# Output stores on ScalarE's queue and an exchange of two head pairs in the ramp: an attention and SwiGLU kernel on one core

## The chip, the cores and the metric

The kernel runs on one core of one Trainium2 chip. The metric is the device time of one execution in microseconds (us). A measurement here is six executions of a kernel, one of them with the profiler, beside eleven of the kernel before on the same chip in the same rounds (six in the first measurement of the change).

## The reference, cut to what matters

```python
# q, k, v: (8 batches, 8 heads, 576, 64); blocks of 64; w_gate, w_val: (512, 1536); w_out: (1536, 512)
scores = where(block_i >= block_j, q @ k.T / sqrt(64), -1e9)      # block-causal
attn   = softmax(scores) @ v
x      = attn as (4608 tokens, 512)
xn     = x / sqrt(mean(x * x) + 1e-6) * rms_g
out    = (silu(xn @ w_gate) * (xn @ w_val)) @ w_out                # (4608, 512) float32
```

## The kernel before

The kernel interleaves the feed-forward part of one batch with the attention of the next. The order of all work is written in strings of short names. In them `t0` to `t3` are the transposes of batch 1's head pairs on TensorE (called PE below), `a0` a set of value matmuls, `Z` a matmul of zeros whose result nobody reads and that only keeps PE busy, `U` a tile of gate or value projections, `O` a third of a down projection, `f0` to `f4` the transposes of the normalized activations by DMA, `l` a load and `p` a transpose of Q and K by DMA. In the code and in the profile, `ob` is the scaled output tile, and its scaling pass on ScalarE is called an ob below.

```python
RAMP = """
...
e3 D02 Z Z n0 Z n1 nr D11 D10 Z nx t3 Z a0 p D22 Z D12 D23 Z D20 a1 D21 D31 t0 D32 a2 D33 D30
... """
SECOND = """
... U l u1 f1 B1 u0 f0 O O C1 u2 f2 u3
f3 O l l p V00 V01 A2 l p u4 f4 V11 O V10 B3 l l l O O l l V21 l l C3 V20 z U U U U
"""
```

Each engine runs its own queue in order. SyncE (SP) issues the DMA transposes of Q and K (into tile QKT), those of the activations (XS into XT) and the output stores. A store is 128 rows of 2 KB, and there are 36.

```python
def prep(b, hp):
    ...
    sp(nc.sync.dma_start_transpose(out=T, in_=QKN[b % 2][:, hp, :, :]))       # line 258

# in Norm
def dma(self, j):
    ...
            sp(nc.sync.dma_start_transpose(out=xt(i)[:, :, lo - a:hi - a],    # line 444
                                           in_=self.XS[lo - g0:hi - g0, j, :]))

def down(i, s, part):
    ...
    for m in range(part * 4, part * 4 + 4):
        mm(po, HT[:, m, s * P:(s + 1) * P], WO[:, m, :], m == 0, m == NMC - 1)
    if part == 2:
        ob = obuf.tile([P, DM], FP32, name="ob")
        act_.mul(out=ob, in_=po, mul=0.5)
        held.discard(outs[i, s][0])
        r0 = chunks[i][0] + s * P
        sp(nc.sync.dma_start(out=out[r0:r0 + P, :], in_=ob))                  # line 557
```

A helper records all compute operations, so that in the profile all VectorE (DVE) and ScalarE (ACT) work carries line 116, all matmuls line 122 and all GpSimd loads line 102. Tiles tell them apart.

The softmax here doesn't subtract the row's maximum and nothing guards it: scores larger than these inputs give would overflow.

## Time and profile before

| | before |
|---|---|
| time, median of the first 3 executions | 377.88 us (376.99 to 378.12) |
| span of the profiled execution | 377.1 us |
| PE busy | 363.1 us, 96% |
| PE's longest DMA waits | HT 1.3 and 1.1 us (about 18 us), XT 0.5 us (82 us) |
| SyncE's queue waiting for ScalarE's ob | 123.9 us |
| mean granted clock of PE | 0.994 |

PE is the bound. A lower mean clock means that PE ran some microseconds at half speed. One stretch of 3.3 us at 0.5 lowers the mean over 377 us by 3.3 x 0.5 / 377 = 0.0044. Most of what is missing in 0.994 is one such stretch, the one at 20.8 us that the prediction shows.

### The profile page before, as it was taken

The page shows a single profiled execution, that of the slowest core. Times are in us where ns is not written, and L with a number is a line of the kernel's source. Part 1 is how long each engine was busy: PE and PEld are TensorE (multiplying, and loading weights), DVE is VectorE, ACT ScalarE, POOL GpSimd, SP SyncE. Part 2 cuts the span into 40 slices and gives each one's busy share as a digit, 9 for nine tenths or more (in the row PEclk, how much of TensorE's full clock was granted, in tenths as well). Part 3 has the DMA queues.
Part 4 walks back from the last instruction along what each step waited for, and adds up shares of the span by engine and source line. Part 5 has one row for each costly group of instructions (what it writes and reads, how often), then busy time and mean ns, then how long its engine had stood idle before and what let it go on. Part 6 is the DMA issues. An engine that isn't in the chain of part 4 may idle for free.

```text
span 377.1 us, 7796 instructions
## 1 busy us (share of the span) xinstructions
PE 363.1 (96%) x2953; PEld 188.3 (50%) x2993; DVE 248.9 (66%) x635; ACT 212.8 (56%) x368; POOL 138.7 (37%) x193
## 2 busy tenths in 40 slices
PE   8789999989999999999999999999999999999996
PEld 3458668645455445544454435544554444444442
DVE  6646867878875697648954894569668806724750
ACT  3967767865667657656683668267754313313321
POOL 8653697894887819446805000000000000000000
PEclk9989999999999999999999999999999999999999
DMA  9999999999999999998999427042101320011002
GB/s 161 183 202 200 183 142 158 154 168 142 167 133 185 181 92 137 178 138 84 133 152 95 95 49 141 30 98 42 51 30 28 92 83 29 2 55 56 2 20 92
DMA packets 158519, 41.12 MB, mean 109 GB/s; under 512 B 145169, under 2 KB 153873, under 8 KB 158482
## 3 DMA queue, kind: packets, MB, share of 16 engines
q0 software_dynamic: 103488, 18.59, 67.4%
q1 hardware_dynamic: 54258, 21.74, 28.9%
q8 instruction: 23, 0.38, 0.4%
q10 hardware_dynamic: 736, 0.30, 0.4%
q14 instruction: 14, 0.11, 0.1%
HBM read 37.75 MB, written 9.44 MB: 125 GB/s over the span
## 4 chain that ended last, share of the span: by engine, by line
PE 68%; DVE 14%; DMA 7%; issue 5%; ACT 3%; POOL 2%; DVEq 0%; ACTq 0%; POOLq 0%
PE f L122 63%; PE s L122 4%; DVE HT L116 4%; DVE th L116 3%; DVE XS L116 3%; DMA QKT<-QKN 3%; DMA HT<-in_q_dram 3%; POOL HT L102 1%; DMA XT<-XS 1%; ACT PT L116 1%; DVE XN L116 1%; DVE a L116 1%; ACT th L116 1%; ACT sq L116 1%; POOL VN L102 1%
## 5 line engine op out<-in xcount | busy, mean ns | idle before, releaser
L122 PE MATMUL f<-XT,WG 128*128 128x512 bf16 (+1 forms) x461 | 109.5, 357 | 2.2 <-DVE HT L116 0.6
L122 PE MATMUL f<-XT,WV 128*128 128x512 bf16 (+1 forms) x474 | 110.0, 357 | 1.0 <-DVE HT L116 0.6
L116 ACT ACTIVATE th<-f 128x512 f32<-128x512 f32 x108 | 64.6, 598 | 78.9 <-PE f L122 77.6
L116 ACT ACTIVATE PT<-s 128x1024 bf16<-128x1024 f32 (+2 forms) x100 | 95.6, 992 | 22.4 <-PE s L122 18.7
L116 DVE SCALAR_TENSOR_TENSOR th<-th,f 128x512 f32<-128x512 f32 x108 | 73.9, 684 | 48.1 <-ACT th L116 47.5
L122 PE MATMUL f<-WO,HT 128*128 128x512 bf16 x419 | 99.1, 379 | 1.0
L116 DVE TENSOR_TENSOR HT<-th,f 128x512 bf16<-128x512 f32 x108 | 74.1, 686 | 14.0 <-PE f L122 5.7
L122 PEld LDWEIGHTS <-WV 128*128 128x128 bf16 x480 | 46.8, 98 | 47.3 <-issue 1.3
L122 PEld LDWEIGHTS <-WG 128*128 128x128 bf16 x480 | 45.7, 98 | 45.4 <-issue 3.1
L122 PEld LDWEIGHTS <-HT 128*128 128x128 bf16 x432 | 40.7, 98 | 47.4 <-DVE HT L116 3.0
L102 POOL DMA_DIRECT2D QKN<-in_k_dram x60 | 47.0, 784 | 24.4 <-DMA QKT<-QKN 8.7
L102 POOL DMA_DIRECT2D QKN<-in_q_dram x60 | 47.0, 783 | 13.0 <-DMA VN<-in_v_dram 4.3
L116 ACT ACTIVATE ob<-f 128x512 f32<-128x512 f32 x36 | 21.5, 598 | 48.0 <-PE f L122 48.0
L102 POOL DMA_DIRECT2D VN<-in_v_dram x48 | 38.5, 861 | 19.6 <-PE f L122 17.1
L122 PE MATMUL f<-VN,PT 128*128 128x65 bf16 x960 | 37.8, 194 | 1.5 <-DVE XN L116 0.4
L122 PEld LDWEIGHTS <-PT 128*128 128x128 bf16 x960 | 34.5, 98 | 9.0 <-issue 2.2
L116 DVE TENSOR_TENSOR XN<-f,rd 128x320 f32<-128x320 f32 (+2 forms) x64 | 31.5, 491 | 2.2
L116 DVE MEMSET PT<- 64x64 uint32 (+1 forms) x116 | 11.4, 114 | 27.5 <-ACT PT L116 25.3
L116 DVE SCALAR_TENSOR_TENSOR XS<-XN,y,grow 128x512 bf16<-128x512 f32 x38 | 27.5, 748 | 0.4
L116 ACT ACTIVATE sq<-XN 128x512 bf16<-128x512 f32 x38 | 23.8, 627 | 2.0 <-DVE XN L116 1.7
L122 PE MATMUL s<-QKT 64*128 64x512 bf16 (+4 forms) x240 | 21.9, 294 | 0.0
L116 DVE RECIPROCAL rd<-f 128x5 f32<-128x5 f32 (+2 forms) x64 | 12.1, 190 | 13.0 <-PE f L122 11.6
(54 smaller groups left out, 132.3 us busy)
## 6 DMA issues: line engine op xcount, KB each, us to landing
out_dram<-ob SPq DMA_DIRECT2D x36, 256.0 KB, 2.3
VN<-in_v_dram POOLq DMA_DIRECT2D x32, 128.0 KB, 5.5
QKN<-in_k_dram POOLq DMA_DIRECT2D x48, 64.0 KB, 4.5
QKN<-in_q_dram POOLq DMA_DIRECT2D x48, 64.0 KB, 4.4
WG<-in_moe_w_gate_dram POOLq DMA_DIRECT2D x4, 384.0 KB, 10.4
WV<-in_moe_w_val_dram POOLq DMA_DIRECT2D x4, 384.0 KB, 11.0
WO<-in_moe_w_out_dram POOLq DMA_DIRECT2D x2, 768.0 KB, 11.2
XT<-XS SPq DMA_TRANSPOSE x39, 3.7
```

The lines of the kernel that those rows point to most:

```text
L102: return chain("POOL", nc.gpsimd.dma_start(**kw))
L116: return lambda *a, **kw: chain(self.key, f(*a, **kw))
L122: pe(nc.tensor.matmul(dst, w, r, start=start, stop=stop))
```

## The change

Its intent: SyncE should no longer stand behind stores that wait for ScalarE, and the transposes that waited for the second half of batch 1's keys and queries should find their data.

```diff
-    e3 D02 Z Z n0 Z n1 nr D11 D10 Z nx t3 Z a0 p D22 Z D12 D23 Z D20 a1 D21 D31 t0 D32 a2 D33 D30
+    e3 D02 Z Z n0 Z n1 nr D11 D10 Z nx t0 Z a0 p D22 Z D12 D23 Z D20 a1 D21 D31 t3 D32 a2 D33 D30
...
-            sp(nc.sync.dma_start(out=out[r0:r0 + P, :], in_=ob))
+            act_.dma_start(out=out[r0:r0 + P, :], in_=ob)
```

## The prediction

> **What bounds the kernel now.** I read in this order: the page's busy shares, a table of busy time by stretch, the list of waits (PE's, then the DMA queue's own), then the timelines of the stretch in which PE waits. First the busy shares and the granted clock of the page (before):
>
> ```profile
> PE 363.1 (96%) x2953; PEld 188.3 (50%) x2993; DVE 248.9 (66%) x635; ACT 212.8 (56%) x368; POOL 138.7 (37%) x193
> ...
> PEclk9989999999999999999999999999999999999999
> ```
>
> PE is busy 96% of 377.1 us, so any change has 14.0 us of PE idle to gain from. Where it lies (table by stretch: bounds, length, busy time of each engine with its instruction count, granted clock, DMA share, GB/s):
>
> ```profile
> 17.30:20.80 3.50, 1.12 (x27) 0.75 (x27) 2.81 (x13) 2.22 (x4) 1.89 (x3) 0.99 1.71 184
> 20.80:24.10 3.30, 3.30 (x37) 1.95 (x35) 0.75 (x2) 1.51 (x3) 3.18 (x5) 0.50 1.33 206
> 24.10:44.00 19.90, 19.25 (x286) 15.56 (x286) 13.00 (x29) 15.35 (x28) 9.02 (x12) 1.00 1.37 199
> 44.00:82.00 38.00, 36.41 (x443) 24.24 (x445) 29.31 (x97) 28.93 (x49) 33.12 (x45) 1.00 1.96 153
> 82.00:291.00 209.00, 206.22 (x1594) 100.86 (x1623) 150.13 (x394) 129.19 (x229) 78.16 (x107) 1.00 1.05 110
> 291.00:373.50 82.50, 81.81 (x373) 37.06 (x379) 42.51 (x63) 24.36 (x42) 0.00 (x0) 1.00 0.14 47
> ```
>
> From 82 us to the last matmul PE idles 2.78 + 0.69 = 3.5 us of 291.5: the steady part is PE-bound. One hole stands out: 2.4 us idle in 17.3 to 20.8, then 3.3 us at a clock of 0.50. PE's longest waits and the DMA queue's largest name the two things that the change touches:
>
> ```profile
> PE f L248 <- DMA HT<-in_k_dram: 1.3, 1, 1.3
> ...
> PE f L248 <- DMA HT<-in_q_dram: 1.1, 1, 1.1
> ```
>
> ```profile
> SPq L557 <- ACT ob L116: 123.9, 23, 22.9
> ```
>
> The first two are the transposes of batch 1's last head pair ("t3"), which wait for the second half of batch 1's K and Q. The third: SyncE's in-order queue stood 123.9 us behind output stores that waited for ScalarE's ob. But no line of PE's waits names QKT, and one (0.5 us at 82 us) names XT, the two things that SyncE's queue brings in.
>
> **What the Trainium skill says.** (1) "TensorE: Matmul & The Clock Gate", Part 1: after about an idle window of 3.4 us the array runs at half clock, and as long a busy window brings it back. The trace agrees: 0.50 for 3.3 us after the 3.5 us in which PE was 32% busy; 24 value matmuls took 1.52 us there and 0.90 us at full clock. (2) "DMA: Bandwidth & Descriptors", Issuing engines are not separate DMA queues: another issuing engine saves only the sequencer's issue time. The trace agrees as far as it goes: a store's issue took 332 ns (median) on SyncE, and its transfer landed 2.3 us after. (3) "Perfetto Trace Analysis", DMA Instruction — HWDGE: the recorded span of an issue ends when the sequencer is free for its next instruction, so this time is lost to the engine that issues. (4) "ScalarE: Activation LUTs", What ACT_TABLE_LOAD costs: back-to-back activations overlap by about 93 ns. The trace shows 0.60 us long ones that start 0.49 us apart, so 0.11 us; a store that must see its ob written cannot overlap.
>
> **The change, part by part.**
>
> *Transposes.* The program now runs t0 at t3's old place and t3 at t0's. All other PE instructions keep their place, so what matters is what ends PE's wait there. PE's timeline:
>
> ```profile
> 16.94 0.39 PE L122 MATMUL f<-zeros 128*128 128x512 bf16 x1
> 18.63 0.45 PE L248 MATMUL f<-ident,HT 96*64 96x96 bf16 x12 [1.30 <-DMA HT<-in_k_dram]
> 20.15 0.45 PE L248 MATMUL f<-ident,HT 96*64 96x96 bf16 x12 [1.08 <-DMA HT<-in_q_dram]
> 20.53 0.45 PE L122 MATMUL f<-zeros 128*128 128x512 bf16 x1
> 20.78 1.52 PE L122 MATMUL f<-VN,PT 128*128 128x65 bf16 x24
> ```
>
> GpSimd's timeline of the loads (start, time to write the descriptors, tile and source), then, from the view of tile VN in that stretch, the time from issue to landing of the load that starts at 10.84:
>
> ```profile
> 10.18 0.73 POOL L102 DMA_DIRECT2D HT<-in_q_dram  x1
> 10.84 0.96 POOL L102 DMA_DIRECT2D VN<-in_v_dram  x1
> ```
>
> ```profile
> DMA to landing us min/median/max: 10.0/10.0/10.0
> ```
>
> t0 needs the first half, issued at 8.17 and 8.85 and landed 8.0 and 8.3 us later, at 16.2 and 17.2. So at 17.33 t0 finds its data and both waits are gone: 24 transposes at full clock (0.70 us) end near 18.0, not at 20.6. That looks like 2.4 us, more with the clock. But the next piece, the 24 value matmuls that stood at 20.78, reads V: its third matmul needs V block 2, issued at 10.84 behind the last Q half and landing 10.0 us later, at 20.84; the tail blocks (issued 11.7 and 12.3, landing after 9.3 and 8.9) at 21.0 and 21.2. Before, PE came to that third matmul at about 20.9, just after the landing, so no wait is recorded. After, PE comes at about 18.5 and stands until about 20.9. Gain of the swap: 20.9 - 20.9 = 0, give or take 0.1 us. PE is about as idle in that window (32% before; 0.7 + 0.25 + 0.1 = 1.1 us of 3.5 after), so I keep the half clock too. Moving t3 to 26 us costs nothing new: same 24 transposes.
>
> *Stores.* Removed: 36 issues from SyncE and the hop ScalarE to SyncE (ob ends at 374.08, the last issue starts at 374.10: 0.02 us at the end). Added to ScalarE: 36 issues. A like load, 288 KB, took 428 ns to issue on ScalarE and 399 on SyncE, so 332 x 428/399 = 0.36 us each (estimate), plus the lost overlap of 0.11 and a 0.02 hop: 0.49 x 36 = 17.6 us, ScalarE from 212.8 to 230 us, 61% of the span. What of it meets PE depends on the pause after each ob (ScalarE's timeline, first early in the kernel, then in a steady batch):
>
> ```profile
> 107.75 0.60 ACT L116 ACTIVATE ob<-f 128x512 f32<-128x512 f32 x1
> 108.25 1.94 ACT L116 ACTIVATE PT<-s 128x1024 bf16<-128x1024 f32 x2
> ...
> 192.90 0.60 ACT L116 ACTIVATE ob<-f 128x512 f32<-128x512 f32 x1
> 193.74 1.94 ACT L116 ACTIVATE PT<-s 128x1024 bf16<-128x1024 f32 x2 [0.25 <-PE s L122]
> 195.57 0.23 ACT L116 ACTIVATE PT<-f 128x64 bf16<-128x64 f32 x1
> ```
>
> At 192.90 the store ends near 193.50 + 0.02 + 0.36 = 193.88, so the exps come 0.16 us late, and the tail exp ends at 195.96 instead of 195.80; its bank is taken again by the gate matmuls of 196.01. That is the tightest place of a steady batch: 0 to 0.1 us of PE, five batches, about 0.3. At 107.75 there is no pause at all: 0.49 us late, of which I charge 0.2. The other two obs of a batch stand before squares or a pause of 0.7 us and more, and in the last 83 us obs are 2.6 us apart with 2.0 us of pause: nothing. Freed SyncE: transposes of QKT go out up to 13 us earlier, for which PE never waited: 0. A store that goes out at 74.5 instead of 79.87 now shares the engines with the XT transposes for which PE waits at 82.02: 0 to 0.4 us more, charge 0.1.
>
> Sum: 0 + 0.3 + 0.2 + 0.1 - 0.02 = +0.6 us on 377.88, less a little because such small delays often fall into PE's own slack: 378.3 us.
>
> **Rivals.** (a) The swap is worth its wait: PE keeps its lead and the half-clock window goes (3.3 us at half is 1.65). For: both waits do vanish. Against: V block 2. Even if V came early, the second half of WO caps it: issued at 33.14, landed 12.1 us later at 45.24, and PE needs it at 45.35 + 6 x 0.216 = 46.65, so at most 1.4 us: 376.5. If only the clock window falls well, the same cap holds. (b) Freed SyncE is the gain: 123.9 us of its queue. For it: transposes behind stores feed the chain of waits (QKT and XT, together about 4% there). Against: PE has no QKT wait and idles 1.3% after 82 us; at best 1 us: 377. (c) ScalarE's issues land on the path: if a third of the 17.6 us met PE, 384. Against: pauses of 0.7 to 2.9 us after most obs; I give it 2%. (d) A store on ScalarE waits for an older transfer of its semaphore slot and holds up exps. In the built order those are transfers issued long before, so nothing.
>
> **Range and chances.** The runs before spread over 1.1 us. Low end: clock luck or rival (a) at its cap, less noise, 376.8; high end: each steady batch loses 0.3 us, XT 0.4, 379.9. Two per cent is 7.6 us: a gain of it exceeds half of all PE idle (1%), a loss needs rival (c) (2%); within 2%: 97%.
>
> **What would show it.** In the new profile: no wait of L248 for HT at 17 us, and a new one of 2 to 2.5 us of VN matmuls for VN at about 18.5, ended at 20.9; clock 0.50 after it; the O matmuls starting at 45.2 to 45.5; SyncE's queue without the ob wait; ScalarE issues of 0.33 to 0.45 us; PE idle between 82 and 373 us of 3.5 to 4.5 us. I am wrong if the value matmuls at 18.5 run through, if O starts before 44.5, or if PE's wait for ACT grows by over 2 us.

## The result

The changed kernel took 382.42 us (median of six, 381.16 to 383.80) against 378.00 us (376.61 to 379.58): ratio 1.0120, 95% interval 1.0084 to 1.0156. Ratios here are the mean time of one kernel's executions over that of the other's in the same rounds, so they are not quite the ratios of the medians quoted. By the 2% line this is as predicted, but 382.4 lies outside the range of 376.8 to 379.9. Two repeats, below, gave 1.0091 and 1.0054. The mean of the three ratios is 1.0088, or 3.3 us. The first measurement was the slowest of the three, but even so the cost is several times the 0.4 us predicted.

The profiled execution of the changed kernel spans 382.0 us. The page's busy shares, to be held against those that the prediction shows:

```profile
PE 365.1 (96%) x2953; PEld 188.7 (49%) x2993; DVE 249.3 (65%) x635; ACT 213.4 (56%) x368; POOL 138.7 (36%) x193
```

No engine has more work: the 2 us more of PE are the same matmuls at a lower clock, and ScalarE's issues are not counted as busy. The table by stretch (bounds, length, busy time and count of PE, PEld, DVE, ACT, POOL, granted clock, DMA share, GB/s):

```profile
17.30:20.80 3.50, 1.53 (x40) 1.16 (x40) 3.07 (x13) 2.67 (x4) 1.92 (x4) 1.00 1.71 183
20.80:24.10 3.30, 3.30 (x48) 1.89 (x45) 0.75 (x2) 2.05 (x5) 2.73 (x4) 0.70 1.31 204
...
82.00:87.00 5.00, 3.63 (x9) 1.44 (x11) 2.01 (x6) 1.32 (x3) 4.35 (x7) 0.66 1.71 165
82.00:295.80 213.80, 209.31 (x1594) 101.56 (x1623) 150.40 (x394) 129.64 (x229) 79.44 (x109) 0.99 1.00 110
295.80:378.30 82.50, 81.81 (x373) 37.06 (x379) 42.57 (x63) 24.41 (x42) 0.00 (x0) 1.00 0.12 41
```

The same view of the kernel before, for the one stretch that the prediction does not show:

```profile
82.00:87.00 5.00, 4.93 (x23) 2.29 (x25) 3.59 (x8) 2.51 (x5) 3.78 (x7) 1.00 1.75 163
```

The ramp is as it was: PE is idle about 2 us of the first stretch and at a reduced clock in the next. At 82 to 87 us something is new: PE idles 1.4 us and then runs slowly, at a clock of 0.66. From 82 us to the last matmul PE idles 4.49 + 0.69 = 5.2 us, above the 3.5 to 4.5 us predicted.

The lines of PE's waits that name V and XT, after and then before:

```profile
PE f L122 <- DMA VN<-in_v_dram: 2.0, 1, 2.0
PE f L122 <- DMA XT<-XS: 1.9, 1, 1.9
```

```profile
PE f L122 <- DMA XT<-XS: 0.5, 1, 0.5
```

The VN wait is the one that the prediction expected in place of the two of the transposes. PE's timeline after shows it (start, length, engine, line, operation, count, and in brackets the idle time before it with its releaser):

```profile
18.25 0.23 PE L122 MATMUL f<-VN,PT 128*128 128x65 bf16 x2
20.44 0.82 PE L122 MATMUL f<-VN,PT 128*128 128x65 bf16 x22 [1.97 <-DMA VN<-in_v_dram]
```

Two value matmuls run, the third waits for V block 2, as reasoned. The O matmuls further on start at 44.75 us (before 45.35), but now wait 0.42 us for the down weights, and the first ob starts at 48.13 us (before 48.15): what the exchange gains in the ramp is lost there. The XT wait is the surprise. PE's timeline at that place, before and then after:

```profile
82.02 1.02 PE L122 MATMUL f<-XT,WG 128*128 128x512 bf16 x3 [0.52 <-DMA XT<-XS]
```

```profile
83.23 1.57 PE L122 MATMUL f<-XT,WG 128*128 128x512 bf16 x3 [1.92 <-DMA XT<-XS]
84.60 1.91 PE L122 MATMUL f<-XT,WV 128*128 128x512 bf16 x4
```

PE waits 1.4 us longer, and then four matmuls take 1.91 us instead of 1.03: half clock. The part of the page on DMA issues says who issues the stores now, and the DMA queue's own waits say that SyncE waits for new work (here an XT transpose for VectorE) where it stood behind stores:

```profile
out_dram<-ob ACTq DMA_DIRECT2D x36, 256.0 KB, 2.4
```

```profile
SPq L444 <- DVE th L116: 106.0, 9, 24.9
```

What made XT late? SyncE's timeline before, then ScalarE's and SyncE's after:

```profile
73.25 6.52 SPq L444 DMA_TRANSPOSE XT<-XS  x5
79.87 0.54 SPq L557 DMA_DIRECT2D out_dram<-ob  x1
```

```profile
74.39 0.34 ACTq L116 DMA_DIRECT2D out_dram<-ob  x1
```

```profile
73.07 7.25 SPq L444 DMA_TRANSPOSE XT<-XS  x5
```

Before, SyncE's order held the third store (rows 256 to 383, its ob scaled at 73.8 us) behind five transposes. After, ScalarE sends it at 74.39, among them. The five issues then take 7.25 us instead of 6.52, and XT comes later. This became the first theory. To have a measure that does not depend on how early a run got to this place, I take the gap from the start of the third scaling pass (ob) to the first matmul on XT: before 82.02 - 73.82 = 8.20 us, after 83.23 - 73.75 = 9.48 us.

### The profile page after: what moved, and what is told of

It is laid out like the page before. It is cut to its first block, busy times and chain, and to the rows that moved or that the text cites. A ratio compares the mean times of both kernels' runs of the same rounds, so it can differ in the third digit from the quotient of the medians.

```text
span 382.0 us, 7758 instructions
## 1 busy us (share of the span) xinstructions
PE 365.1 (96%) x2953; PEld 188.7 (49%) x2993; DVE 249.3 (65%) x635; ACT 213.4 (56%) x368; POOL 138.7 (36%) x193
## 4 chain that ended last, share of the span: by engine, by line
PE 57%; DVE 19%; DMA 11%; issue 5%; ACT 5%; POOL 2%; ACTq 0%; DVEq 0%; POOLq 0%
PE f L122 54%; DVE HT L116 6%; DVE th L116 6%; DVE XS L116 3%; DMA WV<-in_moe_w_val_dram 3%; DMA WO<-in_moe_w_out_dram 3%; PE s L122 3%; DMA HT<-in_q_dram 2%; ACT sq L116 2%; DVE a L116 1%; POOL HT L102 1%; DMA XT<-XS 1%; ACT th L116 1%; DVE y L116 1%; DVE XN L116 1%
```

## The experiments

Theory: the stores cost everything and the exchange nothing; the largest part is the third store's data among the transposes that PE waits for, with half-clock stretches behind it, and the rest is ScalarE's issue time in the five batches with the steady order, ahead of what is called the tail's exponential here: the small one of 128x64 behind a pair of large ones. Rivals: the exchange moves loads and so delays XT; every ScalarE issue costs alike; the freed SyncE moves transposes and loads to a bad place.

Results are medians of six; "clock" is the mean of the mean granted clocks of the six executions; "gap" is the measure just explained, from the one profiled execution.

| run | median us | ratio to before (95%) | clock | gap us |
|---|---|---|---|---|
| changed kernel, first | 382.42 | 1.0120 (1.0084 to 1.0156) | 0.991 | 9.48 |
| changed kernel, e5 | 381.43 | 1.0091 (1.0054 to 1.0128) | 0.993 | 9.53 |
| changed kernel, e14 | 380.11 | 1.0054 (1.0014 to 1.0094) | 0.996 | 8.98 |
| stores only, e1 | 380.75 | 1.0066 (1.0035 to 1.0097) | 0.995 | 8.97 |
| stores only, e13 | 381.60 | 1.0084 (1.0049 to 1.0120) | 0.993 | 9.68 |
| exchange only, e2 | 378.48 | 1.0006 (0.9979 to 1.0033) | 0.995 | 8.09 |
| changed, third store on SyncE, e3 | 379.51 | 1.0034 (1.0010 to 1.0058) | 0.997 | 8.24 |
| before, third store on ScalarE, e4 | 379.45 | 1.0050 (1.0010 to 1.0090) | 0.994 | 9.12 |
| e4 and the exchange, e16 | 380.82 | 1.0047 (0.9999 to 1.0095) | 0.993 | 9.43 |
| before and a tiny ScalarE transfer, e6 | 380.66 | 1.0063 (1.0041 to 1.0085) | 0.997 | 7.90 |
| changed, six stores on SyncE, e9 | 378.99 | 1.0015 (0.9974 to 1.0056) | 0.994 | 8.39 |
| changed, third store issued later, e10 | 379.53 | 1.0026 (0.9989 to 1.0064) | 0.996 | 7.74 |
| changed, filled waits, e11 | 380.49 | 1.0059 (1.0023 to 1.0096) | 1.000 | 10.10 |
| changed, filled XT wait, e15 | 380.61 | 1.0061 (1.0031 to 1.0091) | 0.995 | 9.10 |
| exchange, V block 2 early, e7 | 377.47 | 0.9981 (0.9960 to 1.0002) | 0.999 | 8.53 |
| exchange, filled V wait, e8 | 377.46 | 0.9981 (0.9958 to 1.0004) | 0.999 | 8.43 |
| the same, e12 | 377.43 | 0.9972 (0.9934 to 1.0011) | 1.000 | 8.10 |

All outputs are right.

### One part alone: e1 and e2

The stores without the exchange:

```diff
 kernel before
-            sp(nc.sync.dma_start(out=out[r0:r0 + P, :], in_=ob))
+            act_.dma_start(out=out[r0:r0 + P, :], in_=ob)
```

> The kernel before with all 36 stores on ScalarE and the head pairs not exchanged. Theory (the stores cost all of the 4.4 us): 381.5 to 383, PE's wait for the transposed activations at about 83 us is 1.5 to 2.1 us long instead of 0.5, and TensorE runs at about half clock for some microseconds after it. Rival one (the exchange, by the later loads that follow from it, delays the transposed activations): 378 to 379.5, with the wait still near 0.5 us. Rival two (the two parts only hurt together): below 379.5 here and in the exchange alone.

It took 380.75 us, 2.5 us over before by the ratio. That is less than expected. The gap was 8.97 us, PE's XT wait 1.51 us, and no half clock followed it in the profiled execution.

The exchange without the stores:

```diff
 kernel before
-    ... nx t3 Z a0 ... D31 t0 D32 ...
+    ... nx t0 Z a0 ... D31 t3 D32 ...
```

> The kernel before with only the exchange of the two head pairs. Theory: 378.0 plus or minus 0.6, the wait on the transposes' inputs replaced by a wait of about 2 us on the third value block, and what PE gains there lost again at the wait for the down weights. Rival one (the exchange is the cause): 380 or more, with the GpSimd loads of batch 3 later by over 1 us and a longer wait at 82 us.

It took 378.48 us, ratio 1.0006. The exchange costs nothing and gains nothing, and the gap stays short.

### The third store: e3 and e4

```diff
 changed kernel (e3)                                    kernel before (e4): the same with r0 != 2 * P
-            act_.dma_start(out=out[r0:r0 + P, :], in_=ob)
+            if r0 == 2 * P:
+                sp(nc.sync.dma_start(out=out[r0:r0 + P, :], in_=ob))
+            else:
+                act_.dma_start(out=out[r0:r0 + P, :], in_=ob)
```

> The changed kernel with one store of the 36, the third (rows 256 to 383, ready at about 74 us), back on SyncE behind the transposes of the activations; the other 35 stay on ScalarE. Theory (that store's data goes among the transposes PE waits for at 82 us): the wait is back near 0.5 us, no half clock at 84 to 87 us, and the time falls by 2 to 3 us to 379.3 to 380.5. Rival (all 36 issues on ScalarE cost alike, about 0.12 us each): 382.2, unchanged.

> The kernel before with that one store alone on ScalarE, the other 35 on SyncE. Theory: the wait at 82 us grows to 1.5 to 2 us with a half-clock stretch after it, and the time rises by 2 to 3 us to 380 to 381. Rival (the cost is spread over all stores, or comes from SyncE being free for earlier transposes and loads): 378.0 to 378.4.

Taking this one store back brought the changed kernel to 379.51 us, the gap to 8.24 and PE's XT wait to 0.84. Moving this one store alone made before slower by a ratio of 1.0050, and the gap 9.12, which PE's timeline of e4 shows:

```profile
83.47 1.02 PE L122 MATMUL f<-XT,WG 128*128 128x512 bf16 x4 [1.48 <-DMA XT<-XS]
```

Its time, 379.45, was under the 380 to 381 expected, because I had put a half-clock stretch after the wait into the sum, and the profiled execution had none. In e4's trace nothing is lost after that place: from the fifth ob to the last one its distance to before stays the same within 0.06 us.

### Is it the store's data or its issuer: e6 and e10

e6 gives ScalarE the issue time of a store but not the store's data, and leaves SyncE as it was:

```diff
 kernel before
+            act_.dma_start(out=crumbs[:, r0 // P:r0 // P + 1], in_=ob[:, 0:1])
             sp(nc.sync.dma_start(out=out[r0:r0 + P, :], in_=ob))
```

> The kernel before with all stores on SyncE as they were, and after each scaling pass a second, tiny transfer (one column, 128 x 4 bytes, into an SBUF tile nobody reads) issued by ScalarE. It has ScalarE's issue time and none of the store's data, and SyncE's queue is as before. Theory: no growth of the wait at 82 us (0.4 to 0.8 us), 0.17 us more in each of the five batches at the exponential of the tails, and 0.3 to 0.5 in the batch from 164 to 190: 379.2 to 379.8. Rival (SyncE being freed, and with it the earlier transposes and loads, costs what is not the third store's): 378.0 to 378.5 and no 0.17 us steps.

The gap is 7.90 us: an issue by ScalarE without the data does not delay XT. The time, 380.66 us, was above what I expected, for a reason that helps: this tiny transfer took 472 ns to issue (median), the real store 338 ns. In the five batches the steps at the tail's exponential were 0.30 to 0.33 us each (read from the start of the next ob, against the exchange-only kernel) instead of 0.16 to 0.18 in e3. An issue longer by 0.13 us makes a step larger by about as much, so there is no slack at that place.

e10 keeps all 36 stores on ScalarE, but issues the third one about 5 us later:

```diff
 changed kernel
-    ... A2 l p u4 f4 V11 O V10 B3 l l l O O ...
+    ... A2 l p u4 f4 V11 O V10 B3 L l l l O O ...      # L: issue the third store now, on ScalarE
-            act_.dma_start(out=out[r0:r0 + P, :], in_=ob)
+            if r0 == 2 * P:
+                later.append((r0, ob))
+            else:
+                act_.dma_start(out=out[r0:r0 + P, :], in_=ob)
```

> The changed kernel, all 36 stores on ScalarE, but the third is issued about 5 us later in ScalarE's order, at about 80 us, behind the exponentials that follow its scaling pass and shortly before the fourth. Theory (what costs is the store's data among the transposes, whoever issues it): from that scaling pass to the first matmul on the transposed activations it is 8.0 to 8.6 us instead of 9.0 to 9.5, and the time is that of the kernel with the third store on SyncE, ratio 1.003 to 1.005. Rival (a store issued by ScalarE costs there because of the engine or its queue): 9.0 to 9.5 us, ratio 1.006 to 1.010.

SyncE's five transposes and PE's first matmul on them:

```profile
73.15 6.41 SPq L444 DMA_TRANSPOSE XT<-XS  x5
```

```profile
81.70 1.02 PE L122 MATMUL f<-XT,WG 128*128 128x512 bf16 x4 [0.30 <-DMA XT<-XS]
```

The transposes take 6.41 us again, and the gap is 7.74 us, the shortest of all. So it is neither ScalarE nor its queue that delays XT, but the time at which the store's data travels. (What the store and the transposes contend for was not isolated.) The ratio of 1.0026 is a little under the 1.003 to 1.005 that I expected.

Over all traces the two groups do not overlap. With the third store sent at about 74 us (nine traces) the gap is 8.97 to 10.10 us, mean 9.38, and the five transposes take 6.89 to 7.28 us to issue. With it sent later (nine traces: before, e2, e3, e6, e7, e8, e9, e10, e12) the gap is 7.74 to 8.53 us, mean 8.18, and the issues take 6.41 to 6.78 us. The third store's place costs 9.38 - 8.18 = 1.2 us. In e9 the GpSimd loads of the next values began 8.3 us after the third ob, later than in any other of these traces (in the changed kernel 6.6 us), and the gap was 8.39: the rival that makes late loads the cause falls.

### The other stores: e9

```diff
 changed kernel
-            act_.dma_start(out=out[r0:r0 + P, :], in_=ob)
+            if r0 // P in (2, 6, 9, 13, 17, 21):       # the third, and the five ahead of a tail exponential
+                sp(nc.sync.dma_start(out=out[r0:r0 + P, :], in_=ob))
+            else:
+                act_.dma_start(out=out[r0:r0 + P, :], in_=ob)
```

> The changed kernel with six stores back on SyncE: the third, and the five that stand on ScalarE directly before a pair of exponentials and the exponential of the tails (the 7th, 10th, 14th, 18th and 22nd); 30 stay on ScalarE. Theory (each of the five holds the tail's exponential up by a store's issue, and so a bank that PE wants back): the 0.17 us steps at these five places are gone, 0.85 us less than the kernel with 35 stores on ScalarE (which was 1.0034 of before): 1.000 to 1.002, 378.4 to 379.0. Rival (every store on ScalarE costs its bit, whichever place it has): 1.0025 to 1.003, about 379.3.

378.99 us, ratio 1.0015, in the middle of what was expected, though the interval is too wide to exclude the rival by itself. The trace does exclude it: at these five places the kernel with 35 stores on ScalarE loses 0.16 to 0.18 us each against the exchange-only kernel, and e9 loses nothing (it gains up to 0.06 us).

How a store's issue gets there is seen at the 14th ob. ScalarE's timeline after (the prediction shows the same place of before, at 192.90):

```profile
197.05 0.60 ACT L116 ACTIVATE ob<-f 128x512 f32<-128x512 f32 x1
197.68 0.34 ACTq L116 DMA_DIRECT2D out_dram<-ob  x1
198.06 1.94 ACT L116 ACTIVATE PT<-s 128x1024 bf16<-128x1024 f32 x2 [0.41 <-PE s L122]
```

VectorE clears the masked blocks behind these exponentials. VectorE and PE before, then VectorE and PE after:

```profile
195.75 0.19 DVE L116 MEMSET PT<- 64x64 uint32 x2 [0.80 <-ACT PT L116]
```

```profile
197.74 1.07 PE L122 MATMUL f<-VN,PT 128*128 128x65 bf16 x30
```

```profile
200.07 0.19 DVE L116 MEMSET PT<- 64x64 uint32 x2 [0.80 <-ACT PT L116]
```

```profile
201.92 1.14 PE L122 MATMUL f<-VN,PT 128*128 128x65 bf16 x30
```

The exponentials start 1.01 us after the ob instead of 0.84, so 0.17 us late. VectorE's clear then comes 3.02 us after the ob instead of 2.85, again 0.17 late, and the next ten VectorE instructions, which follow each other almost without a pause, keep 0.16 to 0.17 us of this lateness. PE loses 0.04 us up to the matmuls at 201.06 (4.01 us after the ob instead of 3.97). The other 0.13 us it loses in the 30 value matmuls: the next instruction starts 203.04 - 201.92 = 1.12 us behind their start, before 198.73 - 197.74 = 0.99, and in e9 0.93. Which of VectorE's instructions those value matmuls wait for was not isolated (a PSUM bank that VectorE has still to read is likely).

### Do the two parts hurt together: e5, e13, e14, e16

```diff
 e5, e14: the changed kernel, unedited
 e13: stores only (e1), unedited
 e16: e4 with the exchange of t0 and t3
```

> The changed kernel once more, unedited, on the chip of the next three runs. The single parts gave 0.2 us for the exchange, 1.9 (about 1.0 at equal clock) for the third store and about 1.4 for the other 35, so if they add up it is 380.5 to 381.5, and the 382.4 of the first measurement held more half-clock stretches than usual. If the exchange and the stores hurt only together it is 382 or more again at the same granted clock.

> All 36 stores on ScalarE without the exchange, unedited repeat on the chip of the next three. If the exchange and the stores interact: ratio 1.005 to 1.008 again, and 8.9 to 9.2 us from the third scaling pass to the first matmul on the transposed activations. If the difference was chance: as the changed kernel beside it, within 0.002.

> The changed kernel, a third measurement. Interaction: ratio 1.009 to 1.012, 9.4 to 10.1 us from the third scaling pass to that matmul, and a mean granted clock lower by about 0.003 than the stores alone. Chance: within 0.002 of the stores alone.

> The kernel before with the exchange and the third store alone on ScalarE; the other 35 on SyncE. Interaction of these two: 9.4 us or more from scaling pass to matmul, ratio 1.006 to 1.008. No interaction: 8.9 to 9.2 us, ratio 1.003 to 1.005.

After e1 to e5 the parts seemed to sum to less than the whole (2.5 + 0.2 us against 4.5 and 3.4), and the gaps were longer with the exchange. Side by side on one chip it came the other way round: stores only 1.0084 and a gap of 9.68, changed kernel 1.0054 and 8.98. That is 0.0030 apart, so it met neither what was expected of an interaction nor the 0.002 expected of chance. e16's ratio fits no interaction, its gap of 9.43 alone would have fitted one. So the difference was most likely chance, and this is visible if executions are sorted by their granted clock.

The table counts every execution whose clock was recorded (before's six in the first measurement have none). It pools four rounds on chips 2, 3 and 7 and the first measurement; before's means within a class differ between the four rounds by up to 0.5 us in the first two columns and 1.0 us in the third.

| executions with a clock of | 0.997 or more | 0.992 to 0.996 | under 0.992 |
|---|---|---|---|
| before (44) | 15, mean 377.23 us | 20, 378.41 us | 9, 379.98 us |
| changed kernel (18) | 4, 379.61 us | 6, 381.07 us | 8, 382.83 us |
| stores only (12) | 3, 379.66 us | 7, 381.32 us | 2, 382.97 us |

Along a row the columns stand for about zero, one and two half-clock stretches, and each costs 1.2 to 1.8 us. Down a column the changed kernel and the stores alone are equal within 0.25 us, and both are 2.4 to 3.0 us above before. The first measurement of the change had no execution of the first class among its six.

### The half-clock stretches: e8, e12, e11, e15

If PE's idle time brings them, then idle-time matmuls that fill a wait should take them away and cost nothing.

```diff
 e8, e12: before with the exchange, and
-    ... nx t0 Z a0 ...
+    ... nx t0 Z Z Z Z Z Z Z Z a0 ...
 e11: the changed kernel with that, and
-    ... C3 V20 z U U U U
+    ... C3 V20 z Z Z Z Z Z Z U U U U
 e15: the changed kernel with the second edit alone
```

> The kernel before with the exchange and seven more of the kernel's own idle-time matmuls (zeros times zeros, 0.22 us each) between head pair 0's transposes and the value matmuls that wait. They lie in the wait, so they cost nothing if the wait is over 1.5 us, and TensorE is not idle in front of the stretch at 21 to 24 us. Theory: no half clock there, granted clock 0.999 or 1.0 in most executions, 377.0 to 377.4 (what the fast executions of before without a half-clock stretch take). Rival: the half clock comes whatever PE does there: 378 to 378.6 with clocks of 0.995.

> The fill before the value matmuls on the kernel with stores on SyncE once more, to narrow its interval: 0.9981 again (0.997 to 0.999), clocks 0.998 to 1.0.

> The changed kernel with idle-time matmuls (zeros times zeros) in its two longest waits: seven more before the value matmuls at 18 us and six before the first matmul on the transposed activations at 82 us. The waits end when they did, but TensorE is not idle in them. Theory (about 1 us of the change's 3.5 to 4.4 is half-clock stretches that follow the longer waits): granted clock 0.998 to 1.0 in most executions instead of 0.986 to 0.995, and 379.4 to 380 us, ratio 1.003 to 1.005. Rival (half clock unconnected with PE's idle time): clocks of 0.99 and ratio 1.009.

> The changed kernel with six idle-time matmuls only in the wait at 82 us, none in the ramp. Theory: the half-clock stretch at 84 to 87 us is gone and that of the ramp stays; mean granted clock 0.994 to 0.996, as that of the kernel before, and a ratio lower by about 0.003 than the changed kernel beside it. Rival (the stretch comes whatever PE does): as the changed kernel.

The stretch at 20.8 us of e8, in the columns used above:

```profile
20.80:24.10 3.30, 3.30 (x60) 2.04 (x56) 1.00 (x4) 2.42 (x5) 2.68 (x4) 1.00 1.32 204
```

All 18 executions of e8, e12 and e11 have a clock of 0.998 or more, where of before 15 of 44 have 0.997 or more. So the stretches follow PE's idle time, at least its longest waits. In e15, with only the XT wait filled, all six have 0.993 to 0.995: one stretch, that of the ramp, and never two.

The gain is less clear than the clock. e8 and e12 are 377.35 us on average, before in their rounds 378.23: 0.88 us less, with a standard error of 0.29. But e11 took 380.49, over the 379.4 to 380 expected, and e15 was no faster than the changed kernel beside it (1.0061 and 1.0054), where I expected 0.003 less. In e11's profiled execution the gap was the longest of all, 10.10 us. That gap is where its time went: the profiled executions of e11 and e14 both have a clock of 1.0 and differ by 380.35 - 379.17 = 1.18 us, of which 1.12 lie in the gap. PE still waited 1.08 us for XT behind the fill, so the fill did not stand in the way; XT itself came late. Why it did, one trace each with the fill (10.10 and 9.10) does not tell.

### V block 2 early: e7

```diff
 kernel before with the exchange, and in the order of the first loads
-    ... Ka Qa Kb Qb v2 vt ...
+    ... Ka Qa v2 vt Kb Qb ...
```

> The kernel before with the exchange, and the loads of value block 2 and of the value tail put ahead of the second halves of batch 1's keys and queries, which the exchange no longer needs early. Theory of the ramp: the value wait of about 2 us at 18 to 21 us is gone; 0.5 to 1.4 us faster than before (376.6 to 377.7), more if the half-clock stretch that follows it goes too. Rival: the load only moves the wait to the down weights at 46 us: 378 to 378.5.

377.47 us, ratio 0.9981, all six clocks 0.998 or more. The V wait is gone, and PE waits 0.81 us for the down weights at 45 us instead. This is what the prediction had said of the exchange: it is worth something only if V comes earlier, and the down weights cap it. None of e7, e8 and e12 is shown to beat before by its own interval. The two of the fill together are the best candidate, by about 0.9 us.

## Why the prediction was right or wrong

**The exchange: 0. Right.** The waits of the transposes gave way to one for V block 2, 1.97 us long, which ended at 20.44 us (predicted 2 to 2.5 us, ended at 20.9). The exchange alone measured 1.0006. That PE's clock would be lowered behind it held in the profiled execution (0.70 instead of the 0.50 forecast, then 0.82 up to 28 us), but it is not a fixed property: before and after, some executions have that stretch and some have none. The prediction treated it as fixed. One sign missed: the O matmuls started at 44.75 us and not at 45.2 to 45.5. The zero therefore rests not on V alone but also on the down weights, which the prediction had only as the cap of its rival (a).

**XT: "0 to 0.4 us more, charge 0.1". This step failed.** The mechanism was named rightly: a store that goes out at 74.5 instead of 79.87 us shares the engines with the transposes of XT. The size was wrong. It measured 1.2 us, shown by e3, e4, e6 and e10. What these runs show of the mechanism is that the time of the store's data counts; that the two contend for the engines stays inferred. In the changed kernel PE had little to hide it behind, since it already waited 0.5 us for the same transposes in the kernel before. Where an engine already waits, no slack is left to take a delay up.

**The steady batches: 0 to 0.1 us in each of five batches, 0.3 together. The size was wrong.** It was 0.17 us in each, 0.83 together in e1. The exponentials came 0.16 us late by the prediction (its own sum, 193.88 - 193.74, gives 0.14) and 0.17 by the trace. But the prediction followed this only to the tail's exponential and its bank, where PE indeed lost just 0.04 us at the 14th ob. It did not follow the delay into VectorE's queue, which runs almost without a pause there; behind it the value matmuls lose the remaining 0.13 us. e6 showed that there is next to no slack at this place.

**"The other two obs of a batch stand before squares or a pause ...: nothing." Wrong in part.** Between the 12th and 13th ob (166 to 187 us in before) e1 lost 0.38 us, the changed kernel 0.83 in its first profile, and e6, with SyncE as before, 0.37. Store issues ahead of the squares make VectorE's root of the norm later. There small VectorE instructions were also longer: y took 0.17 us in the kernel before and 0.58 in e3, and x, which took 0.17 in before, took 0.46 in e1:

```profile
173.12 0.17 DVE L116 TENSOR_SCALAR y<-x 128x5 int32<-128x5 int32 x1
```

```profile
172.33 0.58 DVE L116 TENSOR_SCALAR y<-x 128x5 int32<-128x5 int32 x1
```

```profile
173.48 0.46 DVE L116 TENSOR_SCALAR x<-ss 128x5 f32<-128x5 f32 x1
```

GpSimd issues loads at that time, in e3 since 168.2 us, in before only since 173.05, which is 0.07 us ahead of y. The Trainium skill ("SBUF — State Buffer", Who interferes with whom) says that tensor_scalar can take a two-port mode, and that then whichever of GpSimd and VectorE issues first blocks the other for its whole instruction. The traces fit this but do not isolate it: only x and y, the two tensor_scalar operations of the root, were long (0.23 to 0.70 us instead of 0.17 in some batches, of before too), and the other small operations beside them kept 0.17. In before y overlapped a load and still took 0.17, so an overlap alone does not lengthen it. How the loss divides can be read from the kept traces. In all eleven in which ScalarE issues the stores (or e6's tiny transfers) ahead of the squares, x starts 0.13 us late after the 12th ob (0.26 in e6), x and y together last 0.12 to 0.74 us longer, and the 13th ob is late by the sum of the two less 0.04 to 0.06 us. In e1 that is 0.13 + 0.29 against 0.38. In the seven traces without those issues both kept 0.17 in this batch. At the remaining obs e1 lost 0.19 us in sum.

**0.2 us at 107.75. Wrong, it was 0.** In e1 the fifth, sixth and seventh ob keep the same distance to before (0.06 us).

**Freed SyncE: 0. Right**, as far as e6 shows: with SyncE's queue unchanged, ScalarE's issues alone make all the steps after 90 us. (PE's idle share after 82 us in its argument, 1.3%, should read 1.2: 3.5 of 291.5 us.) **Issue time:** estimated 0.36 us, measured 0.34.

**Not in the sum: more half-clock stretches.** Of before's executions 20% have a clock under 0.992, of the changed kernel's 44%. Changed minus before is 381.53 - 378.33 = 3.2 us over all executions, and 2.4 to 2.9 within a class, so this part is some 0.5 us. It is uncertain, because e14 beside e13 shows how much six executions vary.

The sum that the runs support: 1.2 us at XT, about 1.5 us in the batches after it (1.33 to 1.90 in the eight traces of kernels with all stores on ScalarE, from the fifth ob to the last: e1, e5, e10, e11, e13, e14, e15 and the first), which is 2.7 us at equal clock, and some 0.5 us of half clock: 3.2 us. Still open are what lengthens VectorE's x and y, which instruction hands the tail's delay on to the value matmuls, and why XT came latest of all in e11, whose six executions are 1 us above the changed kernel's of their clock class.

## What to carry to other kernels

A store moved to another queue is also a store moved in time: ask what its data will meet, above all transfers that an engine already waits for, because there no slack is left to absorb it. Follow a small delay through every in-order queue that it enters, not only to the first buffer that it frees. And sort executions by granted clock before explaining a difference of one per cent, since a single half-clock stretch, 1.2 to 1.8 us, is as large as about half of the difference here.

## What the Trainium skill lacked or had wrong

- "TensorE: Matmul & The Clock Gate", Part 1 and the table of goals, speak of idle windows and gaps of more than about 3 us. Here a half-clock stretch followed a wait of 1.92 us, with PE busy 1.95 of the 4.0 us before 84 us, and with idle-time matmuls in the waits of up to 2 us no such stretch shows in the clocks of 18 of 18 executions. The page says that the number of slow matmuls at a kernel's start varies from run to run; it lacks that executions of one kernel also differ by stretches later on and so fall into classes (377.23, 378.41 and 379.98 us).
- "DMA: Bandwidth & Descriptors", Issuing engines are not separate DMA queues, says that another issuing engine only saves issue time. That the transfers share the engines agrees with e10. It lacks that the move changes the order against the old queue's transfers: 1.2 us here, more than three times the 0.34 us of the issue.
- The same page, DMA Transpose: nothing on the time that a plain store costs a stream of transposes beside it. With one 256 KB store among them five transposes took 6.89 to 7.28 us to issue, without it 6.41 to 6.78 us.
- The same page, Issuing engine by pattern, has no issue times. From an SBUF tile that ScalarE had just written, a transfer of 128 x 4 bytes to another SBUF tile took ScalarE 472 ns to issue (e6), one of 128 x 2 KB to the output in DRAM 338 ns.
